# Loading q in rows of eight tokens and sorting it by 0/1 matmuls, in a decayed attention followed by a two-layer network

## The chip, the cores and the metric

The kernel runs on one core of one Trainium2 chip. A core has TensorE (PE, matmuls; its weight loads are listed apart as PEld), VectorE (DVE), ScalarE (ACT), GpSimd (POOL) and SyncE (SP). Each of them takes its own instructions in order; POOL and SP also issue the transfers between the chip's memory and the core's. The metric is the device time of one execution in microseconds (us). Lower is better.

## The reference

```python
# q, k, v: (4, 8, 768, 64) float32: batch, heads, tokens, head size
gamma = 1.0 - 2.0 ** (-5.0 - np.arange(H))
for t in range(S):
    state = gamma[None, :, None, None] * state + np.einsum('bhd,bhe->bhde', k[:, :, t], v[:, :, t])
    y[:, :, t] = scale * np.einsum('bhd,bhde->bhe', q[:, :, t], state)
x = y.transpose(0, 2, 1, 3).reshape(B * S, H * D)      # (3072, 512)
h = x @ w_in                                           # (512, 2048)
s = np.sin(alpha * h)
out = (h + s * s / (alpha + 1e-09)) @ w_out            # (2048, 512)
```

Each head keeps a 64x64 state that fades by its own gamma. Two matrix products with a squared sine between them follow, over all 3,072 tokens.

## The kernel before

**Tiles and groups.** The tokens are cut into 24 tiles of 128, six for each of the four batches. `order` lists them by the order of work: first the first tile of each batch (places 0 to 3, called first to fourth tile here, and e0 to e3 in the code), then the rest. The first four make group 0, then come eight groups of two, and a last one of four. Inside a tile the attention is a masked, decayed product of q and k; between the tiles of a batch it goes through the state. All matmuls read bfloat16.

**One of the first tiles.** Tokens arrive on partitions, as (token, head, 64). `half_T` (line 273) turns q (TH.n.0) and k (TH.n.1) on PE by four 128x128 transposes each, and CH copies the result out of PSUM into `qkT`. `products` (AA, line 299) multiplies k by q in the `pa` banks, `decayed` (E, line 309) multiplies by the table `dec` on DVE, `mixed` (MM, line 339) multiplies by v, and Y copies the result into `xT`, the input of the network. q and k of the very first tile come as float through SP (line 171) and are cast on DVE (cq) and ACT (ck); everything else is cast by POOL's transfers. The fourth tile has the same steps under the names H.0, H.1, A3 and M3.

**One of the fifth to eighth tiles (places 4 to 7).** `stage_T` (T, line 283) turns q and k by 16 transposes on half the columns each, and C copies them out. `burst` (U.n, line 457) is then one block on PE: tile n's part from the state, its own products, the scores of tile n+1 and the sums for the state. What it leaves on DVE is called exit (into `xT`), keep (the state), mask (of the scores); hand is the state's bfloat16 copy on ACT. From the ninth tile (place 8) on, q and k are turned by a DMA transpose that SP issues (X).

**The network.** A slot S.g:m takes a few of the 16 column blocks of w_in: PE multiplies (line 610), ACT takes the sine (line 613), Q squares it (ACT line 618, or DVE line 620), A writes h + s*s/alpha as `gT` on DVE (line 625). S.e:0 to S.e:3 cover the first three tiles in 384 columns, S.e:4 the same four blocks for the fourth tile in 128; the others of group 0 are 512 wide. F.t.f multiplies gT by one block of w_out into the result of tile t (line 635); O copies that out of PSUM and G sends it.

**What sets the order.** The front, up to the end of group 1's first product, is written out by hand: each word of `PLAN` (line 16) issues one step, and each engine gets its instructions in that order. L loads a tile's q, k or v, K a piece of w_in, W a piece of w_out, all from POOL; x and w are matmuls on zeros that fill PE's time; D makes a decay table on POOL out of `qg`, which gr makes on ACT; V scales v. Later groups are issued by loops that the change doesn't touch.

**Banks.** PSUM has four banks in rotation for most uses (`mm`), a pair for products (`pa`) and a pair called `two`, which holds in turn the first mixed results and alpha (`front`), the fourth tile's turned q and k, the results of the first two tiles (until their O), and the bursts.

## Time and profile before

| | |
|---|---|
| median of 3 runs | 209.41 us (208.93 to 209.41) |
| span of the profiled execution, first to last instruction | 206.7 us |
| PE busy | 200.4 us, 97% |
| DVE, ACT, POOL busy | 154.9, 151.6 and 123.6 us |
| PE in 0 to 5, 5 to 10, 10 to 15, 15 to 20 us | 3.81, 4.51, 4.49 and 4.79 us |
| transfers issued by POOL | 80,080 packets, 13.38 MB |

The profiled execution's own time is given as its span; the difference of 2.7 us to the runs' median lies before its first and after its last instruction. PE counts as busy also while it multiplies zeros: in the first 14 us 54 such matmuls take 8.3 us. A line number is one of the kernel before.

### The profile page before, as it was taken

What the parts mean: (1) busy time and instruction counts of PE and PEld (TensorE: products, weight loads), DVE (VectorE), ACT (ScalarE), POOL (GpSimd) and SP (SyncE); (2) the same over time, 40 slices, a digit from 0 to 9 for tenths busy, and PEclk for the clock granted to TensorE, in tenths of its full rate; (3) what the DMA queues carried; (4) which work ended last, traced back from release to release, by engine and by line L of the source; (5) the groups of instructions that cost most, each with busy time, mean ns of one, the idle gap of its engine ahead of it and who ended that gap; (6) DMA issues with size and microseconds to landing.
All of it is one profiled execution on the core that took longest, in us unless ns stands there. A gap on an engine that the chain in (4) does not pass through costs nothing.

```text
span 206.7 us, 5872 instructions
## 1 busy us (share of the span) xinstructions
PE 200.4 (97%) x2399; PEld 126.2 (61%) x2399; DVE 154.9 (75%) x325; ACT 151.6 (73%) x310; POOL 123.6 (60%) x171
## 2 busy tenths in 40 slices
PE   7999999999999999999999999999999999999993
PEld 7545544467776666666666676766766654444463
DVE  5777499878999988878889686976977875656120
ACT  7778788547897787687687788588687679998001
POOL 8998997999979986699485929972310000000000
PEclk9999999999999999999999999999999999999999
DMA  9999999999999999999994998992423101010212
GB/s 135 147 171 192 200 202 173 167 128 134 246 142 146 101 152 190 167 130 138 189 159 67 125 134 108 142 135 53 105 71 35 54 15 38 3 51 0 102 59 96
DMA packets 102907, 24.81 MB, mean 120 GB/s; under 512 B 93360, under 2 KB 99936, under 8 KB 102880
## 3 DMA queue, kind: packets, MB, share of 16 engines
q0 software_dynamic: 80080, 13.38, 90.1%
q1 hardware_dynamic: 22656, 10.99, 25.5%
q8 instruction: 19, 0.31, 0.6%
q10 hardware_dynamic: 144, 0.07, 0.1%
q14 instruction: 8, 0.07, 0.1%
HBM read 27.30 MB, written 6.29 MB: 163 GB/s over the span
## 4 chain that ended last, share of the span: by engine, by line
PE 87%; POOL 6%; DMA 3%; DVE 1%; ACT 0%; issue 0%; POOLq 0%
PE po L635 39%; PE ph L610 38%; DMA w_out<-in_moe_w_out_dram 3%; POOL qkr L125 3%; POOL vr L125 2%; PE poh L662 2%; PE py L372 2%; PE pa L387 1%; PE pt L290 1%; PE py L445 1%; PE py L436 1%; POOL w_in L161 1%; DVE s L620 1%; PE pa L394 1%; PE pa L420 1%; PE y L436 1%
## 5 line engine op out<-in xcount | busy, mean ns | idle before, releaser
L625 DVE SCALAR_TENSOR_TENSOR gT<-s,rec_alpha,ph 128x256 bf16<-128x256 f32 (+3 forms) x164 | 79.7, 522 | 27.2 <-ACT s L618 26.8
L610 PE MATMUL ph<-xT,w_in 128*128 128x256 bf16 (+3 forms) x656 | 98.3, 291 | 0.0
L613 ACT ACTIVATE s<-ph,alpha_sb 128x256 f32<-128x256 f32 (+3 forms) x164 | 76.1, 507 | 27.1 <-PE ph L610 23.7
L635 PE MATMUL po<-w_out,gT 128*128 128x512 bf16 x368 | 94.6, 379 | 0.1
L610 PEld LDWEIGHTS <-w_in 128*128 128x128 bf16 x656 | 63.2, 98 | 32.7 <-DVE s_f L568 0.5
L618 ACT ACTIVATE s<-s 128x512 f32<-128x512 f32 (+1 forms) x93 | 58.3, 627 | 2.9
L635 PEld LDWEIGHTS <-gT 128*128 128x128 bf16 x368 | 34.3, 98 | 30.2 <-DVE gT L625 0.5
L149 POOL DMA_DIRECT2D qk_seq<-in_q_dram x32 | 21.7, 719 | 5.3 <-DMA v_seq<-in_v_dram 3.9
L149 POOL DMA_DIRECT2D qk_seq<-in_k_dram x32 | 21.3, 706 | 4.7 <-DMA qk_seq<-in_q_dram 4.7
L649 DVE COPY o_sb<-po 128x512 f32<-128x512 f32 x20 | 13.8, 689 | 9.2 <-PE po L635 8.8
L149 POOL DMA_DIRECT2D v_seq<-in_v_dram x24 | 16.9, 782 | 0.0
L188 POOL TENSOR_TENSOR v_seq<-v_seq,kgq 128x512 bf16<-128x512 bf16 x9 | 9.3, 1051 | 4.5 <-DMA v_seq<-in_v_dram 4.5
L125 POOL DMA_DIRECT2D vr<-in_v_dram x11 | 10.3, 939 | 0.9 <-DMA w_in<-in_moe_w_in_dram 0.7
L406 DVE TENSOR_TENSOR aTw<-pa,maskq 128x768 bf16<-128x768 f32 x10 | 9.6, 956 | 0.0
L682 PE MATMUL spare<-warm 128*128 128x112 bf16 (+1 forms) x54 | 8.3, 323 | 1.2 <-DVE warm L198 1.2
L494 DVE TENSOR_TENSOR xT<-py,qg 128x512 bf16<-128x512 f32 x13 | 8.9, 684 | 0.5 <-PE py L452 0.5
L666 ACT COPY o_sb<-poh 128x256 f32<-128x256 f32 (+1 forms) x2 | 0.6, 320 | 11.7 <-PE poh L662 11.7
L520 POOL CAST s_q<-s_f 128x256 bf16<-128x256 f32 x1 | 0.4, 398 | 14.2 <-DVE s_f L514 14.2
L390 DVE TENSOR_TENSOR aT<-pa,mask 128x1024 bf16<-128x1024 f32 x7 | 8.5, 1218 | 0.4 <-PE pa L387 0.4
L520 ACT CAST s_q<-s_f 128x256 bf16<-128x256 f32 x12 | 4.8, 396 | 3.4 <-DVE s_f L514 2.7
L125 POOL DMA_DIRECT2D qkr<-in_k_dram x7 | 6.2, 891 | 0.4 <-DMA w_in<-in_moe_w_in_dram 0.4
L125 POOL DMA_DIRECT2D qkr<-in_q_dram x7 | 6.4, 915 | 0.1
(123 smaller groups left out, 178.3 us busy)
## 6 DMA issues: line engine op xcount, KB each, us to landing
out_dram<-o_sb SPq DMA_DIRECT2D x23, 256.0 KB, 3.1
w_in<-in_moe_w_in_dram POOLq DMA_DIRECT2D x8, 256.0 KB, 8.1
w_out<-in_moe_w_out_dram POOLq DMA_DIRECT2D x8, 256.0 KB, 8.0
vr<-in_v_dram POOLq DMA_DIRECT2D x11, 128.0 KB, 6.5
v_seq<-in_v_dram POOLq DMA_DIRECT2D x16, 80.0 KB, 5.0
qkr<-in_q_dram POOLq DMA_DIRECT2D x7, 128.0 KB, 6.2
qkr<-in_k_dram POOLq DMA_DIRECT2D x7, 128.0 KB, 6.1
qk_seq<-in_q_dram POOLq DMA_DIRECT2D x16, 48.0 KB, 4.5
```

The source lines that it names most:

```text
L125: nc.gpsimd.dma_start(out=t, in_=chunk_of(src, j))
L149: nc.gpsimd.dma_start(out=o, in_=src[bt, head(b, m, e), now[0] * C:(now[-1] + 1) * C, :].rearrange("(f i) d -> i f d", i=64))
L188: eng.tensor_mul(t, t, by[:, j % NCH, :, None].to_broadcast([128, H, D]))
L390: return {"mask": lambda: nc.vector.tensor_mul(aT.rearrange("p e n t -> p (e n) t"), pa.rearrange("p e (n t) -> p (e n) t", n=NP), mask_bc)}
L406: return {"mask": lambda: nc.vector.tensor_mul(aT, pa[:, :, 0:384].rearrange("p e (m t) -> p e m t", m=2), maskq[:, None, None, :].to_broa ...
L494: nc.vector.tensor_mul(o, st["pyw", old][:, :, 0:256].rearrange("p b (m t) -> p b m t", m=2), by)
L610: nc.tensor.matmul(self.ph[:, m, :], w_in[:, i, f * 128:(f + 1) * 128], xT[g][:, i, self.lo:self.hi], start=(m == 0 and i == 0), stop=(i = ...
L613: nc.scalar.activation(out=self.s[:, m, :], in_=self.ph[:, m, :], func=ACTF.Sin, scale=alpha_sb[:, f:f + 1])
L618: nc.scalar.activation(out=self.s, in_=self.s, func=ACTF.Square)
L625: nc.vector.scalar_tensor_tensor(gT[self.g][:, f, self.lo:self.hi], self.s[:, m, :], rec_alpha[:, f:f + 1], self.ph[:, m, :], op0=ALU.mult ...
L635: nc.tensor.matmul(po[g, ts], gT[g][:, f, ts * C:(ts + 1) * C], w_out[:, f, :], start=(f == 0), stop=(f == FF - 1))
L649: nc.vector.tensor_copy(o_sb, po[g, ts])
```

## The change

*Loads.* q of the second to eighth tile (`order[1:8]`) is read so that a partition holds eight tokens of one head, one run of 2 KB in memory, where it held one token of eight heads in runs of 256 bytes: 128 runs for a tile instead of 1,024. v of the first tile is read as float by SP behind q and k, and cast on DVE (cv).

*Sorting.* In that layout a transpose alone would leave the tokens out of order. `rows_T` multiplies each of the eight token rows by columns of the identity, once for even and once for odd heads: 16 matmuls of 64 columns, into a whole bank of float. The copy out of PSUM puts the tokens in order. In `stage_T` q and k now have a bank and a copy each.

*Order and engines.* The zeros are 30 and 9 matmuls instead of 41 and 13. The second and third tile's k is copied by ACT, not DVE; the second tile's Y goes from ACT to DVE; `qg` is one product on DVE (ge) and one exponential on ACT; alpha has a bank of its own, and the second tile's products use `two`. Much of PLAN stands in another order.

```diff
+    in_rows = {("q", j) for j in order[1:8]}
...
+    def rows_of(t, j):
+        b, c = divmod(j, NCH)
+        return t[b, :, c * C:(c + 1) * C, :].rearrange("h (i r) d -> h i (r d)", r=H)
...
-            if name != "v" and spread(j):
+            if (name, j) in in_rows:
+                nc.gpsimd.dma_start(out=t.rearrange("p r d -> p (r d)"), in_=rows_of(src, j))
+            elif name != "v" and spread(j):
...
-    for name, src in (("q", q), ("k", k)):
+    for name, src in (("q", q), ("k", k), ("v", v)):
...
+    def rows_T(j, bank=None, apart=False):
+        if bank is None:
+            bank = psum.tile([128, 512], F32, name="pt", tag="mm", bufs=4)
+        pt = bank.rearrange("p (r h i) -> p r h i", r=H, h=NP)
+        for r in range(H):
+            for e in range(2):
+                if apart:
+                    pick = ident.rearrange("p (m e b i) -> p e b m i", m=2, e=2, b=2)[:, e]
+                    o = pt[half(e), r].rearrange("p (b m) i -> p b m i", b=2)
+                else:
+                    pick, o = ident.rearrange("p (h e i) -> p e h i", e=2, i=16)[:, e], pt[half(e), r]
+                nc.tensor.matmul(o, raw["q", j][:, r, :], pick, start=(r == 0), stop=True, skip_group_check=True)
+        o = st["qkT", j][:, :NP, :].rearrange("p h (i r) -> p h i r", r=H)
+        x = pt.rearrange("p r h i -> p h i r")
+        return lambda by: by.copy(o, x) if by is nc.scalar else by.tensor_copy(o, x)
...
     def stage_T(j, tag):
...
-        for i in range(2):
-            for p in range(NP):
-                for e in range(2):
-                    h = 4 * (p % 2) + 2 * e + p // 2
-                    nc.tensor.transpose(pt[half(e), i * NP + p, :], raw["qk"[i], j][:, h, :], ident)
-        return lambda by: by.copy(qkT, pt) if by is nc.scalar else by.tensor_copy(qkT, pt)
+        of_q = rows_T(j, banks[0], apart=True)
+        pt = banks[1].bitcast(BF16)[:, :512].rearrange("p (h t) -> p h t", h=NP)
+        for p in range(NP):
+            for e in range(2):
+                nc.tensor.transpose(pt[half(e), p, :], raw["k", j][:, 4 * (p % 2) + 2 * e + p // 2, :], ident)
+        return of_q, lambda by: by.copy(qkT[:, NP:], pt) if by is nc.scalar else by.tensor_copy(qkT[:, NP:], pt)
...
-    def grow(p):
-        nc.scalar.activation(out=qg[:, 0, p, :], in_=tio, func=ACTF.Exp, scale=lgp[:, p:p + 1], bias=cscale)
+    def grow():
+        nc.scalar.activation(out=qg[:, 0], in_=qg[:, 0], func=ACTF.Exp, bias=cscale)
+    def exponents():
+        nc.vector.tensor_mul(qg[:, 0], tio[:, None, :].to_broadcast([128, NP, C]),
+                             lgp[:, :, None].to_broadcast([128, NP, C]))
...
-L.0.v L.1.q L.1.k L.1.v L.2.q L.2.k L.2.v K.0.0 K.0.1 tk x.41 cq TH.0.0 CH.0.0.D ck w.2 dm TH.0.1 CH.0.1.A kg st
+L.1.q L.1.k L.2.q L.2.k L.1.v L.2.v x.30.112 K.0.0 K.0.1 tk cq.D TH.0.0 ge CH.0.0.D dm.1 w.1 w.3 kg ck.A dm.0
...
```

POOL's first loads, before (a tile's load is 128 partitions of 8 heads of 64; the last number after x is how often the row comes):

```order
L125 DMA vr<-in_v_dram 128x8x64
L125 DMA qkr<-in_q_dram 128x8x64
L125 DMA qkr<-in_k_dram 128x8x64
L125 DMA vr<-in_v_dram 128x8x64
L125 DMA qkr<-in_q_dram 128x8x64
L125 DMA qkr<-in_k_dram 128x8x64
L125 DMA vr<-in_v_dram 128x8x64
L161 DMA w_in<-in_moe_w_in_dram 128x4x256 x2
```

and with the change:

```order
L128 DMA qkr<-in_q_dram 128x1x512
L133 DMA qkr<-in_k_dram 128x8x64
L128 DMA qkr<-in_q_dram 128x1x512
L133 DMA qkr<-in_k_dram 128x8x64
L133 DMA vr<-in_v_dram 128x8x64 x2
L169 DMA w_in<-in_moe_w_in_dram 128x4x256 x2
```

Six loads stand ahead of w_in instead of seven; two of them are q in rows; both v come after both k.

DVE from q of the first tile to the third tile's xT, before (L779 is the cast of q, L281 a copy of turned q or k, L314 and L317 the decay, L352 Y):

```order
L779 CAST qb<-o_sb 128x512
L281 COPY qkT<-pt 128x512
L788 TENSOR_TENSOR dec<-dec,mask_114 128x1024
L314 TENSOR_TENSOR aT<-pa,dec 128x1024
L281 COPY qkT<-pt 128x512
L234 MEMSET lgq 64x1 x8
L235 TENSOR_TENSOR expoq<-tok,lgq 128x48
L314 TENSOR_TENSOR aT<-pa,dec 128x1024
L281 COPY qkT<-pt 128x512
L317 TENSOR_TENSOR aT<-pa,dec 128x2x256 x2
L352 CAST xT<-front 128x2x128
L352 CAST xT<-pyh 128x2x128
```

and with the change, from behind the cast of q (L724 is ge, L785 the cast of v, L314 a copy, L352 and L355 the decay, L390 Y):

```order
L724 TENSOR_TENSOR qg<-tio,lgp 128x512
L314 COPY qkT<-pt 128x512
L833 TENSOR_TENSOR dec<-dec,mask_117 128x512 x2
L785 CAST vr<-o_sb 128x512
L352 TENSOR_TENSOR aT<-pa,dec 128x1024
L246 MEMSET lgq 64x1 x8
L247 TENSOR_TENSOR expoq<-tok,lgq 128x48
L352 TENSOR_TENSOR aT<-pa,dec 128x1024
L355 TENSOR_TENSOR aT<-pa,dec 128x2x256
L390 CAST xT<-pyh 128x4x128
L355 TENSOR_TENSOR aT<-pa,dec 128x2x256
L390 CAST xT<-pyh 128x2x128 x2
```

The two copies of k have left DVE; ge, a cast and the second tile's Y have come to it, the last between the two halves of the third tile's decay.

DVE around the bursts U.4 and U.5, before (L514 is keep, L390 mask, L649 the copy O.1, L497 and L494 exit):

```order
L514 TENSOR_TENSOR s_f<-s_f,py_712 128x128
L514 TENSOR_TENSOR s_f<-s_f,py_713 128x128
L390 TENSOR_TENSOR aT<-pa,mask_114 128x1024
L649 COPY o_sb<-po 128x512
L497 TENSOR_TENSOR xT<-py_712,qg 128x2x128
L497 TENSOR_TENSOR xT<-py_713,qg 128x2x128
L494 TENSOR_TENSOR xT<-py,qg 128x2x2x128
```

and with the change (L535 and L532 are exit, L552 keep, L428 mask, L687 O.1, L328 the copy of the seventh tile's k, C.k6):

```order
L535 TENSOR_TENSOR xT<-py_759,qg 128x2x128
L535 TENSOR_TENSOR xT<-py_760,qg 128x2x128
L552 TENSOR_TENSOR s_f<-s_f,py_759 128x128
L552 TENSOR_TENSOR s_f<-s_f,py_760 128x128
L428 TENSOR_TENSOR aT<-pa,mask_117 128x1024
L687 COPY o_sb<-po 128x512
L328 COPY qkT<-pt 128x512
L532 TENSOR_TENSOR xT<-py,qg 128x2x2x128
```

The exit of U.4 now stands first instead of behind O.1, and the copy of the seventh tile's k is on DVE behind O.1.

98 lines of the change are left out of this document (58 added, 40 removed).

## The prediction

> **What bounds the kernel now.** I read the table of stretches first (time, then busy time of PE, PEld, DVE, ACT and POOL with their instructions, granted clock, DMA share, GB/s), then the chain of waits, then PE and DVE in order of time.
>
> ```profile
> 20.00:25.00 5.00, 4.93 (x35) 2.80 (x36) 2.09 (x7) 3.89 (x10) 4.98 (x7) 1.00 1.36 200
> ...
> 50.00:60.00 10.00, 9.52 (x174) 7.36 (x172) 9.72 (x22) 8.96 (x21) 10.00 (x14) 1.00 1.86 201
> ```
>
> From 20 us on PE is busy all the time, save 0.48 us after 50. The later part gets shorter only if PE has less to do; the part before 20 us, only if that state begins earlier. What begins it, by the chain of waits (start, length, what):
>
> ```profile
> 13.01 7.02 DMA w_out<-in_moe_w_out_dram
> 20.07 0.81 PE po L635 x3
> ...
> 22.42 3.45 PE ph L610 x16
> ```
>
> Read alone this says loads: the second piece of w_out is issued at 13.01 and lands at 20.03. But the chain names only the last of several. DVE and PE in order of time (start, length, line, operation; in brackets the idle time before, and what ended it) show a second chain that ends as late:
>
> ```profile
> 3.97 0.49 DVE L779 CAST qb<-o_sb 128x512 bf16<-128x512 f32 x1 [0.48 <-DMA o_sb<-in_q_dram]
> ...
> 7.63 1.23 DVE L314 TENSOR_TENSOR aT<-pa,dec 128x1024 bf16<-128x1024 f32 x1 [0.41 <-PE pa L305]
> ...
> 9.83 1.22 DVE L314 TENSOR_TENSOR aT<-pa,dec 128x1024 bf16<-128x1024 f32 x1
> ...
> 12.16 1.29 DVE L317 TENSOR_TENSOR aT<-pa,dec 128x512 bf16<-128x512 f32 x2 [0.50 <-PE pa L305]
> ...
> 13.84 0.43 DVE L352 CAST xT<-pyh 128x256 bf16<-128x256 f32 x1
> ...
> 16.28 0.43 DVE L281 COPY qkT<-fourth 128x512 bf16<-128x512 bf16 x1 [1.10 <-PE fourth L279]
> 16.62 0.61 DVE L625 SCALAR_TENSOR_TENSOR gT<-s,rec_alpha,ph 128x384 bf16<-128x384 f32 x1
> 17.18 0.43 DVE L281 COPY qkT<-fourth 128x512 bf16<-128x512 bf16 x1
> 18.16 1.23 DVE L314 TENSOR_TENSOR aT<-pa,dec 128x1024 bf16<-128x1024 f32 x1
> ```
>
> ```profile
> 1.19 3.77 PEld L682 LDWEIGHTS <-warm 128*128 128x128 bf16 x41 [1.19 <-DVE warm L198]
> ...
> 5.42 0.87 PE L682 MATMUL spare<-warm 128*128 128x512 bf16 x2
> 6.12 0.39 PE L279 MATMUL pt<-ident,kb 128*128 128x128 bf16 x4
> 6.35 0.59 PE L682 MATMUL spare<-warm 128*128 128x512 bf16 x2
> ...
> 14.18 1.46 PE L610 MATMUL ph<-xT,w_in 128*128 128x384 bf16 x8
> 15.84 0.40 PE L279 MATMUL fourth<-ident,qkr 128*128 128x128 bf16 x4 [0.20 <-DMA qkr<-in_q_dram]
> 17.72 0.40 PE L305 MATMUL pa<-qkT 64*128 64x128 bf16 x8
> ...
> 20.72 1.05 PE L610 MATMUL ph<-xT,w_in 128*128 128x128 bf16 x16
> ```
>
> Tiles 0, 1, 2 are decayed on DVE at 7.63, 9.83 and 12.16; xT of the third is whole at 13.84 + 0.43 = 14.27. PE's first two 384-wide slots are through at 15.46 (14.18 + 8 x 0.16). Then the fourth tile's q, its copy, a gT step, the copy of k, products at 17.72, decay at 18.16 to 19.39, mix, xT, and the 128-wide slot S.e:4 at 20.72. The next 512-wide slots need that xT, so an earlier w_out alone wins nothing: S.e:4 must come earlier too.
>
> **The change part by part.** *Loads.*
>
> ```profile
> 1.37 1.07 POOL L125 DMA_DIRECT2D vr<-in_v_dram  x1 [0.17 <-issue]
> 2.44 0.89 POOL L125 DMA_DIRECT2D qkr<-in_q_dram  x1
> ...
> 7.65 1.55 POOL L161 DMA_DIRECT2D w_in<-in_moe_w_in_dram  x2
> ...
> 11.42 0.72 POOL L165 DMA_DIRECT2D w_out<-in_moe_w_out_dram  x1
> ```
>
> A load of 1,024 short rows costs POOL 0.89, w_in's 512 rows 0.78 (1.55 / 2), w_out's 256 rows 0.72; on that line 128 rows cost about 0.69 (bounds: 0.5 and 0.89). v of the first tile leaves POOL. POOL then starts w_in at 1.37 + 0.86 + 0.87 + 0.68 + 3 x 0.87 = 6.39 instead of 7.65 (0.86 is 0.69 plus the 0.17 by which the first issue is dearer), and after the fourth tile's q the lead is 1.26 + 0.2 = 1.46: w_out's second piece lands at about 18.6. Bounds of the lead: 0, if the DMA engines set the pace alone, and 1.5. The new wait of POOL is the decay table D.3 behind K.1.0; it needs qg from ACT (about 12.7 by the chain below; one exponential 512 wide in place of four) when POOL is there (13.0), and behind it stand pieces needed after 20 us. v as float is a third transfer on SP; its cast costs DVE 0.49 as q's does and is read at about 11 us, so even 3 us of delay is covered.
>
> *Sorting.*
>
> ```profile
> L324 PE MATMUL ps<-vr,kb 128*64 128x64 bf16 x8 | 0.3, 195 | 0.0
> L290 PE MATMUL pt<-ident,qkr 128*64 128x128 bf16 x64 | 2.5, 222 | 0.0
> 37.03 0.64 PE L290 MATMUL pt<-ident,qkr 128*64 128x128 bf16 x16
> L281 DVE COPY qkT<-pt 128x512 bf16<-128x512 bf16 x3 | 1.3, 422 | 1.4 <-PE pt L279 1.4
> L649 DVE COPY o_sb<-po 128x512 f32<-128x512 f32 x20 | 13.8, 689 | 9.2 <-PE po L635 8.8 <-ACT o_sb L647 0.4
> L352 ACT CAST xT<-front 128x512 bf16<-128x512 f32 x2 | 1.2, 584 | 0.4 <-PE front L348 0.4
> ```
>
> Per tile q takes 16 matmuls of 64 columns on 128x64 weights instead of 4 (first tiles) or 8 (later) transposes. The nearest row is L324, same weights and columns: 8 in 0.29 of which one takes 0.195, so (0.29 - 0.195) / 7 = 0.0136 each, 0.22 for 16. The eight transposes it replaces in a later tile: L290 ran 16 in 0.64 (one of them 0.222), (0.64 - 0.222) / 15 = 0.028 each, 0.22 for 8. So the later four tiles cost nothing more; the upper bound, 16 at L290's 0.028, is 0.22 a tile, 0.9 in all. I take 0, since L324 has the very shape.
>
> [...]
>
> The copy reads float PSUM across 256-byte steps: on ACT the nearest float row is 0.58, as for bf16; on DVE 0.69 against 0.42. I take these; twice them is the upper bound.
>
> *The chain to the third tile's xT.* Line by line from the new order, with these prices and 0.04 from one engine to the next. q's cast ends at 4.46, and its transposes no longer wait for 41 fillers (until 4.96): they start at 4.50. Four 512-wide fillers instead of two then stand ahead of k's transposes. The filler rows give 0.43 each at 5.42 and about half at 6.35, so PE's pace doubles near 6.0; k's transposes start at 6.35 instead of 6.12. DVE has meanwhile the exponents (0.69), q's copy, the mask of dec in two halves and v's cast (0.49), done by 7.4; they hide in the idle time before its first decay, and lengthen it by what they pass 7.8. Copy on ACT 6.78-7.37, products, first decay **7.85** (before 7.63). q of the second tile: sorted 7.75-8.15, ACT 8.19-8.78, k's copy to 9.26, products from 9.30, second decay **9.74** (9.83). Third tile: q's copy 9.26-9.85, alpha, k's copy 10.08-10.67, products, first half of the decay at **11.15** (12.16): its products no longer wait for a bank, and DVE has given both k copies to ACT. Then Y.1 11.79-12.48, second half 12.38-13.06, Y.2.1 13.44-**13.87** (14.27). PE runs half of S.e:1 early and is through with both slots at **14.87** (15.46).
>
> *The fourth tile.* Its q lands at 15.84 - 1.26 = 14.6, so it no longer waits (15.84: 0.20 for the load). But what comes behind it is late next:
>
> ```profile
> 15.09 0.58 ACT L613 ACTIVATE s<-ph,alpha_sb 128x384 f32<-128x384 f32 x1 [1.32 <-PE ph L610]
> 15.71 0.52 ACT L618 ACTIVATE s<-s 128x384 f32<-128x384 f32 x1
> ```
>
> ACT's order is now sine, sine, square, square: sines at 14.43 and 15.07, squares at 15.69 and 16.20. DVE's H.0 copy 15.31-16.0; gT waits for the square, 16.25; H.1's copy stands behind it in the queue, 16.78-17.21; products 17.25, decay **17.69** (18.16), mix 18.97, xT 20.0, S.e:4 at **20.04** (20.72). Of the 0.68, one F matmul of 0.215 has moved behind S.e:4: gain 0.46. With fillers that cost nothing it would be 0.7; without the lead of the loads, 0.
>
> *From 37 us.* From T.4 to U.5 PE has the same work in both orders: 22 F matmuls, three tiles' transposes, Z's scores, U.4.
>
> ```profile
> 42.27 0.49 DVE L514 TENSOR_TENSOR s_f<-s_f,py 128x128 f32<-128x128 f32 x2 [0.61 <-PE py L452]
> 42.68 1.22 DVE L390 TENSOR_TENSOR aT<-pa,mask 128x1024 bf16<-128x1024 f32 x1
> 44.29 0.69 DVE L649 COPY o_sb<-po 128x512 f32<-128x512 f32 x1 [0.40 <-ACT o_sb L647]
> 44.90 0.75 DVE L497 TENSOR_TENSOR xT<-py,qg 128x256 bf16<-128x256 f32 x2
> ...
> 45.11 0.31 PE L372 MATMUL py<-qkT,s_q 64*64 64x128 bf16 x8
> ...
> 50.83 0.31 PE L372 MATMUL py<-qkT,s_q 64*64 64x128 bf16 x8 [0.48 <-DVE qkT L291]
> ```
>
> Before, U.5 started when O.1's copy had freed its bank (44.29 + 0.69), and the exit of U.4 came after. Now exit (0.75), keep (0.49) and the mask (1.22) stand ahead of O.1's copy, and C.k6's copy behind it: with U.4 4.4 after T.4, O.1's copy ends 8.26 after T.4, C.k6's 8.60; U.5 goes from 8.07 (45.11 less 37.03) to 8.35, and its scores wait 0.1 more. In return T.7 now stands ahead of S.1:1 and S.1:2, and its k copy is half as long: U.6 comes at 13.92 instead of 13.80. So the stall of 0.48 at 50.83 is not gained but moved to U.5: 0.1 lost. If DVE is ahead there by 0.4, it is 0.4 gained. SP's first transpose, X.8, now follows one output instead of standing ahead of three; in the rows above no engine waits for SP, so I cost it at nothing.
>
> **Sum:** -0.46 + 0.1 + 0 (sorting) = -0.36: span 206.7 to 206.35. The median of the runs, 209.41, is 2.7 above the profiled span; I keep that: **209.0**. A change within 0.3% (0.63 us) can't be told from none.
>
> **Rivals.** *The loads decide alone*: S.e:4 follows w_out, and 1.25 to 1.46 of lead arrive. For it: POOL's row of issues without a pause. Against: the chain through DVE has 0.68 less, not 1.4. It decides if ACT's squares and DVE's copies come early. Less 1.3 and 0.1 back: 208.2.
>
> *PE's pace doubles later* (the slower side). PE now rests from 4.0 to 4.5, and this falls into the time in which it was busy without a break before its pace doubled near 6.0. If the doubling comes a like time later, about 9.4: fillers +0.38, k's transposes +0.24, products and the next tile's 16 matmuls +0.2 each, so the second decay comes 1.0 late, and S.e:4 at about 21.1, 0.4 (plus the moved F, 0.2) later than before: 209.4 + 0.6 + 0.1 = 210.1. It decides from the moment the fillers behind q still take 0.43 at 6.1.
>
> [...] The granted clock in the stretches reads 1.00 from the start, so only the spacing shows it here.
>
> *The sorting costs PE what L290's row costs*: 0.9 in the part that PE bounds, after the gain in front: 209.41 - 0.36 + 0.9 = 209.9, no change to tell. For it: weights are loaded 16 times where they were loaded 8 times. Against: L324. [...]
>
> **How the numbers follow.** Forecast as summed 0.45 (own range 208.6 to 209.5, a third of it below 208.78); loads alone 0.22; late doubling 0.18; dear sorting 0.15. Faster: 0.15 + 0.2 + 0.02 = 0.37. Slower: half of the late doubling, and 0.08 from dear sorting with a lost gain: 0.17. The rest 0.46. The range, from the loads' case with 0.4 won at U.5 to the late doubling: 207.8 to 210.2.
>
> **What would show it.** Right: a second decay near 9.7 and a third near 11.2; the fourth tile's q copied before 16.0 with gT behind it near 16.25; S.e:4 near 20.0; w_out's second piece landed near 18.6; U.5 waiting for the copy of O.1 or of C.k6; 24 sorted and transposed instructions in 0.6 us. Wrong: S.e:4 before 19.6 (the loads decide); first decay after 8.3 (the doubling); PE idle time at T.4 and T.5, or more than 0.8 us for their 24 instructions.

## The result

The changed kernel takes 211.87 us (median of four executions, 210.58 to 212.08), the kernel before 209.41 us (208.93 to 209.60) on the same chip. The ratio is 1.012, its interval 1.008 to 1.016: slower, by 2.5 us, where no change was forecast as likeliest. The profiled execution took 211.73 us, with a span of 209.6 us where the kernel before has 206.7. A profile is of one execution, and executions of one kernel here differ by 1 to 2% (25 of the kernel before on one chip 207.69 to 210.22, ten of the version with 41 fillers 209.23 to 213.26), so below the medians say what a kernel takes, and a trace says where.

The same views as before, of the changed kernel. DVE in order of time (start, length, line, operation, then the idle time before and what ended it), up to the fourth tile's decay:

```profile
4.09 0.81 DVE L785 CAST qb<-o_sb 128x512 bf16<-128x512 f32 x1 [0.80 <-DMA o_sb<-in_q_dram]
...
8.93 0.43 DVE L785 CAST vr<-o_sb 128x512 bf16<-128x512 f32 x1 [1.70 <-DMA o_sb<-in_v_dram]
9.28 1.22 DVE L352 TENSOR_TENSOR aT<-pa,dec 128x1024 bf16<-128x1024 f32 x1
...
11.96 1.22 DVE L352 TENSOR_TENSOR aT<-pa,dec 128x1024 bf16<-128x1024 f32 x1 [0.99 <-PE pa L343]
...
13.88 0.69 DVE L355 TENSOR_TENSOR aT<-pa,dec 128x512 bf16<-128x512 f32 x1 [0.70 <-PE pa L343]
...
20.43 1.23 DVE L352 TENSOR_TENSOR aT<-pa,dec 128x1024 bf16<-128x1024 f32 x1
```

PE in order of time:

```profile
1.19 2.98 PE L718 MATMUL spare<-warm 128*128 128x112 bf16 x30 [1.19 <-DVE warm L209]
4.96 0.61 PE L312 MATMUL pt<-ident,qb 128*128 128x128 bf16 x4 [0.79 <-DVE qb L785]
5.36 1.91 PE L718 MATMUL spare<-warm 128*128 128x512 bf16 x4
7.07 0.63 PE L312 MATMUL pt<-ident,kb 128*128 128x128 bf16 x4
8.38 0.61 PE L343 MATMUL pa<-qkT 64*128 64x128 bf16 x8 [0.68 <-ACT qkT L314]
...
13.25 0.59 PE L343 MATMUL pa<-qkT 64*128 64x128 bf16 x8
...
22.82 1.05 PE L648 MATMUL ph<-xT,w_in 128*128 128x128 bf16 x16
```

ACT's cast of k; and on POOL the issue that runs while q is cast, the first piece of w_in, and the load that waits behind it:

```profile
5.95 0.62 ACT L785 CAST kb<-o_sb 128x512 bf16<-128x512 f32 x1 [1.11 <-DMA o_sb<-in_k_dram]
```

```profile
3.72 0.93 POOL L133 DMA_DIRECT2D qkr<-in_k_dram  x1
...
6.34 1.55 POOL L169 DMA_DIRECT2D w_in<-in_moe_w_in_dram  x2
...
9.64 0.91 POOL L133 DMA_DIRECT2D qkr<-in_k_dram  x1 [0.65 <-DMA qkr<-in_k_dram]
```

And the loads of the first 20 us by destination (number, size, median us from issue to landing), before and with the change:

```profile
qkr<-in_q_dram POOLq DMA_DIRECT2D x3, 128.0 KB, 4.8
o_sb<-in_k_dram SPq DMA_DIRECT2D x1, 256.0 KB, 3.9
```

```profile
qkr<-in_q_dram POOLq DMA_DIRECT2D x3, 128.0 KB, 6.8
o_sb<-in_k_dram SPq DMA_DIRECT2D x1, 256.0 KB, 4.7
```

The front lost its time before 17 us. POOL reached w_in at 6.34, as forecast (6.39), but the tiles' q that it loads land 2.0 us later after their issue than before (6.8 for 4.8), k and v 2.4 and 2.1 us. The cast of v waited for its load until 8.93, and the first decay stands right behind it in DVE's queue. In this execution the cast held the decay by little: the products end at 8.99 (8.38 + 0.61), so the decay could have begun near 9.03 at the earliest. PE's fillers still take 0.43 each (1.91 for four) after 5.36, and eight products still take 0.59 at 13.25: PE's pace doubled only behind that.

| start of (us) | before | forecast | with the change | late against before |
|---|---|---|---|---|
| first decay | 7.63 | 7.85 | 9.28 | 1.65 |
| second decay | 9.83 | 9.74 | 11.96 | 2.13 |
| third decay | 12.16 | 11.15 | 13.88 | 1.72 |
| fourth decay | 18.16 | 17.69 | 20.43 | 2.27 |
| S.e:4 | 20.72 | 20.04 | 22.82 | 2.10 |
| T.4 | 37.03 | | 39.34 | 2.31 |
| U.5 | 45.11 | | 48.18 | 3.07 |
| U.7 | 55.26 | | 58.38 | 3.12 |
| last tile's first output product | 199.61 | | 202.99 | 3.38 |

The two stretches that were shown of before (time, busy time of PE, PEld, DVE, ACT and POOL, granted clock, share of the transfers' engines, GB/s):

```profile
20.00:25.00 5.00, 4.95 (x53) 2.84 (x55) 3.13 (x5) 3.34 (x9) 5.00 (x7) 1.00 1.37 199
...
50.00:60.00 10.00, 9.38 (x193) 7.49 (x194) 8.53 (x18) 8.52 (x20) 9.91 (x14) 1.00 1.80 153
```

PE is as full from 20 us on as before (4.95 for 4.93), and has lost 0.14 more in 50 to 60. So 2.1 us of the loss are there at S.e:4, another 0.8 comes between T.4 and U.7. From the last row to the end it takes 0.45 less than before, so the span grows by 2.9. The middle, by engine (PE, then DVE, then POOL in order of time):

```profile
39.34 0.44 PE L297 MATMUL pt<-ident,qkr 128*64 128x64 bf16 x16
39.62 0.39 PE L327 MATMUL pt<-ident,qkr 128*64 128x128 bf16 x8
...
48.18 0.31 PE L410 MATMUL py<-qkT,s_q 64*64 64x128 bf16 x8 [0.60 <-DVE o_sb L687]
```

```profile
43.55 1.78 DVE L199 TENSOR_TENSOR vr<-vr,kg 128x512 bf16<-128x512 bf16 x1
...
47.45 0.67 DVE L687 COPY o_sb<-po 128x512 f32<-128x512 f32 x1
```

```profile
43.67 1.10 POOL L199 TENSOR_TENSOR vr<-vr,kg 128x512 bf16<-128x512 bf16 x1
```

The sorted q and the transposed k of a tile take 0.67 (39.34 to 40.01) for 24 instructions; the 16 transposes before took 0.64. U.5 waits 0.60 for O.1's copy, the wait that the prediction named. The scaling of v at 43.55 is new: it takes 1.78 where 0.69 stood before.

### The profile page after: what moved, and what is told of

It reads as the page before. It is cut to its first block, busy times and chain, and to the rows that moved or that the text cites. A ratio compares the mean times of both kernels' runs of the same rounds, so it can differ in the third digit from the quotient of the medians.

```text
span 209.6 us, 5947 instructions
## 1 busy us (share of the span) xinstructions
PE 198.5 (95%) x2422; PEld 126.6 (60%) x2452; DVE 156.3 (75%) x329; ACT 151.3 (72%) x310; POOL 120.5 (57%) x170
## 3 DMA queue, kind: packets, MB, share of 16 engines
q0 software_dynamic: 73664, 13.25, 82.4%
## 4 chain that ended last, share of the span: by engine, by line
PE 88%; DVE 5%; issue 3%; DMA 2%; ACT 1%
PE ph L648 39%; PE po L673 35%; PE poh L700 2%; DMA o_sb<-in_q_dram 2%; PE py L410 1%; PE spare L718 1%; DVE aT L428 1%; PE pt L297 1%; PE pt L312 1%; PE pa L343 1%; DVE o_sb L687 1%; PE py L474 1%; PE py L483 1%; DVE aT L355 1%; PE pa L425 1%
## 5 line engine op out<-in xcount | busy, mean ns | idle before, releaser
L673 PE MATMUL po<-w_out,gT 128*128 128x512 bf16 x344 | 90.3, 379 | 2.6 <-issue 2.1
L687 DVE COPY o_sb<-po 128x512 f32<-128x512 f32 x20 | 13.7, 687 | 8.8 <-PE po L673 8.8
L133 POOL DMA_DIRECT2D vr<-in_v_dram x10 | 9.1, 912 | 1.0 <-DMA w_in<-in_moe_w_in_dram 1.0
L532 DVE TENSOR_TENSOR xT<-py,qg 128x512 bf16<-128x512 f32 x13 | 8.9, 683 | 0.8 <-PE py L490 0.8
L428 DVE TENSOR_TENSOR aT<-pa,mask 128x1024 bf16<-128x1024 f32 x7 | 8.5, 1216 | 0.0
L718 PE MATMUL spare<-warm 128*128 128x112 bf16 (+1 forms) x37 | 6.3, 357 | 1.2 <-DVE warm L209 1.2
L615 POOL CAST s_q<-s_f 128x512 bf16<-128x512 f32 x2 | 1.4, 702 | 9.6 <-DVE s_f L610 9.6
```

What stands on the lines that cost most here:

```text
L133: nc.gpsimd.dma_start(out=t, in_=chunk_of(src, j))
L428: return {"mask": lambda: nc.vector.tensor_mul(aT.rearrange("p e n t -> p (e n) t"), pa.rearrange("p e (n t) -> p (e n) t", n=NP), mask_bc)}
L532: nc.vector.tensor_mul(o, st["pyw", old][:, :, 0:256].rearrange("p b (m t) -> p b m t", m=2), by)
L673: nc.tensor.matmul(po[g, ts], gT[g][:, f, ts * C:(ts + 1) * C], w_out[:, f, :], start=(f == 0), stop=(f == FF - 1))
L687: nc.vector.tensor_copy(o_sb, po[g, ts])
```

## The experiments

The kernel before has medians of 207.66 to 209.41 in the sets of runs here, which are of several chips, so each kernel is compared with the kernel before on its own chip; the ratio is theirs, with its 95% interval. "S.e:4" and landing times are from the profiled execution of each.

### Fillers and the load of v

From these views I held the pace of PE and the load of v on SP for the causes. Three edits of the changed kernel, alone and together, and one of the kernel before:

```diff
-... L.2.v x.30.112 K.0.0 ...
+... L.2.v x.41.112 K.0.0 ...                     (41 fillers)
-L.1.q L.1.k L.2.q L.2.k L.1.v ...  CH.0.1.A cv.D AA.0.pa
+L.1.q L.1.k L.2.q L.2.k L.0.v L.1.v ...  CH.0.1.A AA.0.pa   (first v by POOL, none on SP)
```

> The changed kernel with 41 narrow fillers again instead of 30, nothing else. Two causes are on the table for the 2.1 us by which S.e:4 came later: PE's pace doubles only near 13 us (the fillers behind q still take 0.43 each, and PE rested from 4.2 to 5.0), and the third float load on SP, which brings k of the first tile 0.8 late and holds DVE's queue until v lands at 8.9. Pace theory: doubling before 8 us, first decay still near 9.3 because DVE waits for v, second near 10.9 instead of 11.96, S.e:4 near 21; median 210.0 to 210.6. SP theory: nothing moves, 211.5 to 212.

> The changed kernel with v of the first tile loaded by POOL as bfloat16 again (behind the second q and k), without SP's float load and DVE's cast; 30 fillers stay. SP theory: k of the first tile is cast at 5.2 instead of 5.95, the first decay comes at 8.0 instead of 9.28 and all behind it 1.2 earlier: 210.3 to 210.8. Pace theory: the cold fillers keep k's transposes at 7.07, the first decay gains only the 0.25 it stood behind v's cast, 211.3 to 211.8.

> Both edits: 41 fillers, and v of the first tile by POOL. If each of the two holds the first decay at about the same time, only both together free it. Both theories: first decay near 7.8, second near 9.8, S.e:4 near 20.2, as the prediction had it; 209.2 to 209.9, with what is lost at U.4 to U.6 (0.8 in the trace). If a third cause is in front, S.e:4 stays after 21 and the time above 210.3.

> The kernel before with 30 narrow fillers instead of 41, nothing else. Pace theory: PE rests before q's transposes, the pace doubles one or two steps later, the second decay moves from 9.83 to past 10.5; 210.2 to 211.5, and runs that differ among themselves by up to 2 us. SP theory: 41 fillers only delayed q's transposes, so no change: 209.2 to 209.6.

Measured: 41 fillers 210.03 us, ratio 1.006 (1.0015 to 1.0105); v by POOL 211.59, 1.013 (1.009 to 1.017); both 209.66, 1.004 (1.001 to 1.007); the kernel before with 30 fillers 209.11, 1.000 (0.997 to 1.004). Neither edit alone mends the change (41 fillers take back about half of the loss), and fewer fillers alone don't harm the kernel before by more than 0.4%. The trace with 41 fillers is of an execution of 212.63, one of the longest of ten; it shows that more fillers don't secure the pace: PE had doubled its pace by 5.4, then rested and lost it again.

```profile
5.39 1.03 PE L718 MATMUL spare<-warm 128*128 128x512 bf16 x4
8.23 0.40 PE L312 MATMUL pt<-ident,kb 128*128 128x128 bf16 x4 [1.81 <-ACT kb L785]
9.31 0.61 PE L343 MATMUL pa<-qkT 64*128 64x128 bf16 x8 [0.68 <-ACT qkT L314]
```

k of the first tile had landed 6.3 us after its issue, PE rested 1.81 us, and from 9.31 on eight products take 0.61.

### Rows of eight tokens in front

A third suspect: the 2-KB rows of q first in POOL's queue hold back SP's 256-byte runs of k. Edits of the version with 41 fillers and v by POOL, the third moving only two scalings of v late in POOL's queue:

```diff
-    in_rows = {("q", j) for j in order[1:8]}
+    in_rows = {("q", j) for j in order[4:8]}       (rows47)
-L.1.q L.1.k L.2.q L.2.k L.0.v L.1.v
+L.0.v L.1.q L.1.k L.2.q L.2.k L.1.v                (vfirst)
-V.6.P L.7.v ...  V.7.P L.10.q L.10.k
+L.7.v V.6.P ...  L.10.q V.7.P L.10.k               (vmoved)
```

> The third version (41 fillers, first v by POOL) with q of the second to fourth tile again in rows of one token; only the fifth to eighth tile are sorted. Theory (2-KB rows ahead in POOL's queue hold back the 256-byte runs of SP's loads): the float k of the first tile lands 3.9 us after its issue, as in the kernel before (4.6 with the rows), its cast starts by 5.3, the first decay by 7.7 (8.05), the third tile's by 11.2 (11.45), the fourth tile's q no longer lands 6.5 us after its issue but near 5, and S.e:4 starts near 20.1; time about 0.4 below the third version. Rival one (it is POOL's order, q and k of two tiles ahead of v, whatever their rows): k lands at 4.6 again, S.e:4 near 20.6, time as the third version's. Rival two (chance from run to run): landing anywhere between 4 and 6.

> The third version (41 fillers, first v by POOL, q of seven tiles in rows of eight tokens) with v of the first tile first in POOL's queue again, as in the kernel before. Theory (2-KB rows hold back the 256-byte runs): part of it stays, since the first rows now start 1.07 later: k lands 4.0 to 4.4 us after its issue (4.6), cast at 5.3 to 5.7. Rival one (POOL's order alone): 3.9, cast at 5.2, first decay by 7.7, the same as before. Rival two (chance): between 4 and 6. Time within 0.4 of the third version's in all cases.

> The third version (41 fillers, first v by POOL, all seven tiles in rows) with POOL's scaling of v of the seventh and eighth tile one load later in POOL's queue each. Theory (a DVE operation with both inputs in SBUF stands still while POOL runs its own TENSOR_TENSOR): in the third version the square on DVE at 49.35 took 1.62 instead of 0.69 beside POOL's scaling at 49.31 to 50.41; moved, the square takes 0.69, the stall of 0.47 ahead of U.6 is gone, U.4 to U.7 takes 13.7 (14.15), and the time is 0.4 below the third version's. Rival (DVE is late there by its own list): the square takes 0.69, yet U.6 waits as long and U.4 to U.7 stays above 14.0.

Measured: without the rows 208.83, 1.0005 (0.997 to 1.004), S.e:4 at 20.36, k landing in 4.2; v first 209.12, 1.003 (1.000 to 1.007), 20.77, k in 4.3; scalings moved 209.40, 1.002 (0.999 to 1.006), 20.59, k in 3.9. The last one has the very front of the version it was made from, where k took 4.6, so k's landing moves from execution to execution, and a difference of 0.7 between two traces proves nothing. Over all traces k takes 3.9, 3.9, 4.2, 4.4 and 3.9 without rows in front and without v on SP, and 4.6, 3.9, 4.3, 5.9, 4.9 and 4.2 with rows: a tendency, not shown.

The moved scalings did what was expected of them. DVE and POOL of the version with 41 fillers and v by POOL, and then DVE with the scalings moved:

```profile
49.35 1.62 DVE L658 TENSOR_TENSOR s<-s 128x512 f32<-128x512 f32 x1 [0.53 <-ACT s L651]
```

```profile
49.31 1.10 POOL L199 TENSOR_TENSOR vr<-vr,kg 128x512 bf16<-128x512 bf16 x1
```

```profile
49.37 0.69 DVE L658 TENSOR_TENSOR s<-s 128x512 f32<-128x512 f32 x1 [0.53 <-ACT s L651]
```

The square takes 0.69 again, no stall is left ahead of U.6 (0.47 before the edit), and from U.4 to U.7 it takes 13.61 us instead of 14.15. The theory is that DVE, with both inputs in SBUF, stands still while POOL runs its own product: in the changed kernel V.5's 1.78 is 0.68 and the whole 1.10 of POOL's. An operation with an input from PSUM kept its length beside POOL's product: the mask at 43.75 took 1.22 in the version with 41 fillers and v by POOL, beside POOL's of 1.04 at 43.54, and 1.22 at 47.60 with none beside it.

### The sorting alone, and the scalings set apart

```diff
 the changed kernel's code and loads of q, with the kernel before's PLAN: 41 fillers,
 L.0.v first, gr as ge on DVE and one exponential; C.4.D becomes C.k4.D C.q4.A, and so on   (order)
-V.6.P L.7.v ...  V.7.P L.10.q ...  (14, (4, 6))
+L.7.v V.6.P ...  L.10.q V.7.P ...  (14, (4, 5))      (apart: in order, and in the kernel before)
```

> The sorting alone: q of the second to eighth tile in rows of eight tokens and its 0/1 matmuls, but the order of the kernel before everywhere: 41 fillers, v of the first tile by POOL and first in its queue, the later tiles' steps where they stood. Theory (sorting is free on PE, and the reordered front with 30 fillers made the loss): first decay at 7.6 to 7.9, S.e:4 at 20.3 to 20.8, from T.4 to U.7 18.0 to 18.3 (before 18.23), time 207.9 to 208.5 where the kernel before has 208.2, ratio 0.998 to 1.002. Rival (rows of eight tokens hold back the other loads, or the sorted copies come late): first decay after 8.0 or S.e:4 after 21.0, ratio 1.003 and more.

> The sorting alone in the old order, and three scalings of v set apart: POOL's of the seventh and eighth tile one load later each, DVE's of the fifteenth tile one step earlier. Theory (a DVE operation on SBUF alone stands still while POOL runs TENSOR_TENSOR): no DVE operation on SBUF alone takes over 0.9 anywhere after 37 us, no stall ahead of U.6, U.4 to U.7 13.3 to 13.5 (before 13.95), time 0.3 to 0.6 below the sorting alone, about 207.7, ratio 0.996 to 0.999. Rival (the coincidences only move): one such operation over 1.2 stays, and the time is within 0.2 of the sorting alone.

> The kernel before with the same three scalings of v set apart and nothing else. Theory: the square on DVE near 48.8 takes 0.69 instead of 1.33, the stall of 0.48 ahead of U.6 is gone, time 0.3 to 0.5 lower, ratio 0.9975 to 0.9985. Rival: U.6 waits as before, ratio within 0.999 to 1.001.

> The changed kernel itself once more, beside the others on this chip and in many executions. Theory (its 30 fillers and the float load of v on SP make the front late in every execution): no time below 210, ratio 1.010 to 1.020, first decay after 9.0, at or behind the cast of v. Rival (chance: k's landing and the doubling of PE's pace fall differently from execution to execution): a third or more of the times below 209.8, ratio below 1.008, or a profile with the first decay before 8.5.

Measured: sorting in the old order 210.94, 1.010 (1.006 to 1.014), far from what I expected; with the scalings apart 210.35, 1.008 (1.005 to 1.011), where I expected 0.996 to 0.999 and no long operation of DVE, yet its square at 50.47 still took 1.48 beside POOL's product at 50.28; the kernel before with them apart 208.24 against 208.44, 0.998 (0.995 to 1.001), not to be told from no change, though its trace has lost the stall of 0.48 ahead of U.6; the change again 211.41, 1.010 (1.005 to 1.016), with one of six executions at 209.70 where I expected none below 210.

The old order doesn't suit the sorting, for a reason that the prediction didn't have. PE in the version "order", at the seventh tile:

```profile
44.48 0.44 PE L297 MATMUL pt<-ident,qkr 128*64 128x64 bf16 x16
45.72 0.41 PE L327 MATMUL pt<-ident,qkr 128*64 128x128 bf16 x8 [0.79 <-ACT qkT L300]
```

A sorted q fills a bank of float by itself, so a tile takes two of the four banks in rotation where both halves shared one. Two of them hold U.4's results until exit.4, which in the old order stands behind O.1; so T.6's k has no bank until ACT has copied T.6's own q, and from U.4 to U.5 it takes 5.0 us, not 3.8. That the bank is what k lacks is read from the kernel's text; the trace shows the wait of 0.79 for ACT's copy. The changed order, with exit.4 first, makes this room, at the price of the wait on O.1: there the 24 instructions of T.6 run without a break. The rest of that version's loss is 0.65 at S.e:4 (k landed in 4.9) and 0.7 at 104 us, where DVE scales v beside POOL; with the scalings apart that last part is gone.

The change once more, in another execution, with k early (5.03) and the pace doubled before 5 us: the first decay waits for v all the same, then PE for the second tile's k and for alpha, and the pace falls back.

```profile
8.56 0.43 DVE L785 CAST vr<-o_sb 128x512 bf16<-128x512 f32 x1 [1.55 <-DMA o_sb<-in_v_dram]
8.90 1.22 DVE L352 TENSOR_TENSOR aT<-pa,dec 128x1024 bf16<-128x1024 f32 x1
```

```profile
9.13 0.40 PE L312 MATMUL pt<-ident,qkr 128*128 128x128 bf16 x4 [1.27 <-DMA qkr<-in_k_dram]
10.71 0.20 PE L854 MATMUL pal<-ident_f,alpha_row 16*128 16x16 f32 x1 [1.18 <-DMA alpha_row<-in_moe_alpha_dram]
10.84 0.64 PE L297 MATMUL pt<-ident,qkr 128*64 128x64 bf16 x16
```

### One part at a time

Landing times told the kernels apart: with v on SP, the q, k and v that POOL loads in front take 6.3 to 7.4 us (medians of each trace), in all others 4.7 to 6.0. Four runs were to show what v on SP, the rows and the fillers do alone:

```diff
 the kernel before:  -for name, src in (("q", q), ("k", k)):   -L.0.v L.1.q     -w.2 AA.0
                     +for ... ("k", k), ("v", v)):             +L.1.q           +w.2 cv AA.0    (v on SP)
 the changed kernel: in_rows of order[4:8]                                      (after_rows47)
 v by POOL, no rows in front, x.30.112                                          (rows47_x30)
 the changed kernel: in_rows of order[4:8], x.41.112                            (rows47_x41)
```

> The kernel before with one edit: v of the first tile leaves POOL and is read as float by SP, third in its queue, and cast by DVE ahead of the first products; 41 fillers, all of q in rows of one token, nothing sorted. Theory (the third float load on SP's queue holds up all loads of the front, as in the three traces that have it: 6.6 to 7.4 us from issue to landing against 4.8 to 6.0 in the others): alpha lands 5.5 to 7 us after its issue (3.8), the second tile's loads 6.5 to 7.3 (4.8 to 5.1), v is cast at 8.2 to 9.0, the first decay starts at 8.6 to 9.4 (7.63), S.e:4 at 21.8 or later (20.72), ratio 1.006 to 1.015. Rival (it is the rows of eight tokens, or the order): landings near 5, v cast by 7.5, first decay by 8.1, S.e:4 by 21.1, ratio below 1.003.

> The changed kernel with q of the second to fourth tile again in rows of one token; float v on SP, 30 fillers and the new order stay. Theory (v on SP): landings of the front stay at 6.5 to 7.4 us, v is cast at 8.2 to 9.0, first decay at 8.6 to 9.6, S.e:4 after 22.0, ratio 1.009 to 1.016 like the change. Rival (the rows of eight tokens in front): k lands in 3.9 to 4.4, the other loads in about 5, first decay by 8.2, ratio below 1.006.

> The version with the first v by POOL and sorting in the fifth to eighth tile alone, with 30 fillers instead of 41. Theory (30 fillers cost something only where loads of the front are late, since PE's rest then grows): k lands by 4.4, first decay by 8.2, S.e:4 by 20.6, time as with 41 fillers (ratio 0.999 to 1.003). Rival (30 fillers alone delay the doubling of PE's pace): fillers still at 0.43 after 6.5, first decay after 8.6, ratio 1.006 and more.

> The changed kernel with q of the second to fourth tile in rows of one token and 41 narrow fillers; float v on SP and the new order stay. It is the last of the eight combinations of fillers (30, 41), v (SP, POOL) and rows in front (yes, no). Theory (30 fillers turn any lateness of the loads into a rest of PE, 41 cover it): the front's loads land 6.3 to 7.3 us after their issue as in every trace with v on SP, yet PE rests less than 1 us between the narrow fillers and k's transposes, first decay 8.2 to 9.2, ratio 1.002 to 1.007, between 1.0155 (30 fillers) and 1.0005 (v by POOL). Rival (v on SP is dear in the new order whatever the fillers): ratio 1.010 and more, S.e:4 after 22.0.

They took 208.78, 211.29, 208.69 and 211.03 us. Loads in the kernel before with v on SP, grouped as above:

```profile
qkr<-in_q_dram POOLq DMA_DIRECT2D x3, 128.0 KB, 6.3
alpha_row<-in_moe_alpha_dram SPq DMA_DIRECT2D x1, 8.0 KB, 5.5
```

The one edit makes the other loads of the front later: q of the next tiles 6.3 us from issue to landing where it was 4.8, alpha 5.5 for 3.8. That half of the theory held. How the loads of the two queues share the transfers' engines was not shown. But the time doesn't follow: ratio 1.001 (0.998 to 1.004). The first decay is 0.40 late (8.03), the second 0.88, S.e:4 only 0.25 (20.97): in the old order most of it is made up.

The three others complete a table of the new order (ratios, with S.e:4 of the trace):

| first v | rows in front | 30 fillers | 41 fillers |
|---|---|---|---|
| SP | yes | 1.012 and 1.010; 22.82 and 23.07 | 1.006; 24.09 (execution of 212.63) |
| SP | no | 1.0155 (1.0095 to 1.022); 23.24 | 1.016 (1.008 to 1.024); 21.34 (and 23.08 with the edit of the last experiment) |
| POOL | yes | 1.013; 21.65 | 1.004; 20.57 |
| POOL | no | 1.0015 (0.998 to 1.005); 21.43 (execution of 209.94) | 1.0005; 20.36 |

Each place is the trace of one execution, and k's landing is in it: 5.9 and 3.9 with v by POOL and 30 fillers, 6.3 in the 24.09. S.e:4 is later with v on SP in all four pairs, by 1.0 to 3.5. Without rows, v on SP is dear with either number of fillers, so my condition (41 cover it) fell, though the last experiment takes 1.0% of the 1.016 away. With v by POOL, no rows and 30 fillers I expected S.e:4 by 20.6; PE was at full pace from 7.81 on there, and waited 1.11 us for a tile's v and 0.75 for the fourth tile's q. What v on SP does where PE's pace is full throughout, with 41 fillers and no rows (DVE, then PE, in order of time):

```profile
8.00 0.59 DVE L785 CAST vr<-o_sb 128x512 bf16<-128x512 f32 x1 [0.95 <-DMA o_sb<-in_v_dram]
8.52 1.20 DVE L352 TENSOR_TENSOR aT<-pa,dec 128x1024 bf16<-128x1024 f32 x1
```

```profile
8.92 0.40 PE L312 MATMUL pt<-ident,qkr 128*128 128x128 bf16 x4 [0.96 <-DMA qkr<-in_k_dram]
...
9.90 0.40 PE L312 MATMUL pt<-ident,qkr 128*128 128x128 bf16 x4 [0.43 <-DMA qkr<-in_q_dram]
...
10.90 0.40 PE L312 MATMUL pt<-ident,qkr 128*128 128x128 bf16 x4 [0.26 <-DMA qkr<-in_k_dram]
...
21.34 1.05 PE L648 MATMUL ph<-xT,w_in 128*128 128x128 bf16 x16 [0.19 <-ACT xT L390]
```

v is cast at 8.00 and the decay stands behind it; then PE waits three times for loads, and S.e:4 is 0.98 later than with v by POOL (20.36). That is the loads' part in this trace.

With 30 fillers and the same loads S.e:4 is at 23.24, and there PE's pace has fallen. Stretches of that trace (time, busy time of PE, PEld, DVE, ACT and POOL, granted clock, share of the transfers' engines, GB/s):

```profile
4.00:7.00 3.00, 1.40 (x10) 0.53 (x8) 2.59 (x5) 1.57 (x6) 3.00 (x5) 1.00 1.70 173
7.00:15.00 8.00, 6.37 (x64) 3.78 (x65) 3.89 (x14) 3.98 (x13) 6.57 (x10) 0.57 2.08 171
15.00:20.00 5.00, 4.35 (x34) 2.39 (x33) 3.84 (x10) 4.78 (x10) 3.98 (x6) 1.00 1.57 192
```

PE had been at full pace at 4.5, rested 1.42 us for k, and had a granted clock of 0.57 over the 8 us from 7 on; if it stood at half in the fall and at 1.00 otherwise, that is an estimated 6.9 us at half (8 x 0.43 / 0.5). S.e:4 is 1.9 us later than in the trace before. The lost pace is the likely reason for most of it; k landed 1.4 us later too (5.3 for 3.9), and no run sets the two apart.

### Keeping PE busy, and the cast later

```diff
 the changed kernel: -dm.1 w.1 w.3 kg   -TH.1.0 w.1 CH.1.0.A TH.1.1 CH.1.1.A
                     +dm.1 w.1 w.7 kg   +TH.1.0 w.5 CH.1.0.A TH.1.1 w.4 CH.1.1.A    (filled)
 and besides         -CH.0.1.A cv.D AA.0.pa   -E.1.- CH.2.1.A
                     +CH.0.1.A AA.0.pa        +E.1.- cv.D CH.2.1.A                  (cast later)
```

> The changed kernel with twelve more 512-wide fillers where PE rested: four ahead of k's transposes, eight around the second tile's; v on SP, 30 narrow fillers, rows and order stay, so the loads are as late as before. Theory (late loads let PE rest for over a microsecond, and then its pace falls back to half): pace stays full from 7 us on (16 sorted matmuls in 0.44, products in 0.40), first decay still at 8.9 to 9.4 behind v's cast, the second at 10.8 to 11.3 (11.96 to 12.37), S.e:4 at 21.3 to 21.9 (22.82 to 23.07), ratio 1.005 to 1.010. Rival (the loads alone set the front): pace full, yet second decay at 11.8 or later and S.e:4 after 22.4, ratio 1.010 and more.

> The same twelve fillers, and v's cast on DVE behind the second decay instead of ahead of the first. Theory (DVE's queue stands behind v's cast): first decay at 8.0 to 8.8, as soon as its products are there, second at 10.0 to 10.8, v's cast by 12.0, S.e:4 0.3 to 0.8 earlier than with the fillers alone, near 21.0, ratio 1.003 to 1.008. Rival (the products are as late as v): first decay within 0.2 of the run with the fillers alone, S.e:4 too.

Measured: 212.59, ratio 1.020 (1.012 to 1.028), and 213.50, 1.024 (1.019 to 1.030). Both missed. The pace was full from 4.4 in the first, but k took 6.2, and eight fillers, 2.1 us, stood ahead of matmuls that could have gone: the second decay came at 13.15. In the second PE had no rest at all between 4.96 and 9.4, and its pace stayed half:

```profile
4.96 0.61 PE L312 MATMUL pt<-ident,qb 128*128 128x128 bf16 x4 [0.80 <-DVE qb L785]
5.37 3.62 PE L718 MATMUL spare<-warm 128*128 128x512 bf16 x8
```

So fillers are no cure: those behind a wait cost what they take, and 4.4 us of work without a break didn't double the pace at once. Whether the later cast helps can't be read from it, since k's transposes, at 8.78, came at the time of v's landing.

### The coincidence at 104 us

The version with v on SP, 41 fillers and no rows had a ratio of 1.016 with only 1.0 us lost at S.e:4. Its trace lost 1.5 us more at one place. DVE and POOL there, and DVE with one scaling moved:

```diff
-    for i, spot in (..., (14, (4, 6))):
+    for i, spot in (..., (14, (4, 5))):
```

> The version before this one (v on SP, 41 fillers, no rows of eight in front) with one edit far from the front: DVE's scaling of the fifteenth tile's v one step earlier. In that version's trace it took 2.78 us at 105.29 instead of 0.68, beside POOL's three scalings from 105.41 on, and the lag against the other traces grew by 1.5 us there. Theory (DVE on SBUF alone stands still beside POOL's TENSOR_TENSOR, and this coincidence is 1.5 of the 2.4 us): the scaling takes 0.7 to 0.9, no lag is added between 95 and 115 us, span about 207.3, ratio 1.005 to 1.011 instead of 1.0161. Rival (the loads in front make all of it, and the coincidence is covered by other work): ratio 1.014 or more.

```profile
105.29 2.78 DVE L199 TENSOR_TENSOR v_seq<-v_seq,kgq 128x512 bf16<-128x512 bf16 x1
```

```profile
105.41 3.56 POOL L199 TENSOR_TENSOR v_seq<-v_seq,kgq 128x512 bf16<-128x512 bf16 x3
```

```profile
104.11 0.91 DVE L199 TENSOR_TENSOR v_seq<-v_seq,kgq 128x512 bf16<-128x512 bf16 x1
```

Measured: 209.50, ratio 1.006 (1.003 to 1.008), from 1.016 (1.008 to 1.024, four executions). The trace is of an execution of 211.26, in which the pace fell back at 11 us, so its span says little; but the scaling takes 0.91, and its steps are as late at 120 us as at 95. The 1.5 us of the one trace are 0.7%, so the fall of 1.0% holds some chance too. What stays, 0.6%, is about the 1.0 us that the front lost in the trace at full pace; in this one S.e:4 came at 23.08.

## Why the prediction was wrong

**The step that failed** is the front's term of the sum, -0.46 with S.e:4 at 20.04. It came at 22.82, 2.10 later than before. Three statements under that term were wrong.

*"read at about 11 us, so even 3 us of delay is covered"*: this counted v's own landing against the first matmul that reads it. It left out two things. The transfer is not alone: as SP's third load it makes the other loads of the front late, 6.3 for 4.8 us in the single edit. And the cast stands on DVE ahead of the first decay. How much that second part costs differs: the first decay began 1.4 us after its products ended in the repeat of the change, 1.0 after with 41 fillers and no rows, 0.3 after in the first trace, and 0.04 after, so not held at all, in three others.

*"PE's pace doubles near 6.0"*: in the first trace of the change it doubled behind 13.25, and there PE made most of the delay: k's transposes began at 7.07 (forecast 6.35) without a rest ahead of them, and the products and all steps up to the third tile's products ran at half pace.

*"q's cast ends at 4.46"*: it took 0.81 instead of 0.49 and ended at 4.90, beside an issue of POOL that lasts to 4.6 in the new order, where one ended at 4.2 before, so the transposes that fewer fillers were to free began at 4.96 and not at 4.50.

**k's landing** was taken as 5.18 without a word. It lands between 3.7 and 6.3 us after its issue in these traces. In the change's first trace its 0.8 of delay cost nothing by itself, since the fillers at half pace lasted longer. In others this and the late loads let PE rest, and in four traces the pace fell behind such rests.

**The late doubling** was a rival with the right side and the right place, at 0.18 and 210.1. Its condition ("the fillers behind q still take 0.43 at 6.1") came true, and pace doubled behind 13.3 rather than at 9.4. It was priced as a delay of the first doubling alone; that a pace once doubled falls back, as in the trace at 10.84, was not in it. Between the run at full pace (S.e:4 at 21.34) and the others with v on SP (22.82, 23.07, and 23.24 without rows) lie 1.5 to 1.9 us, most of them likely pace; the loads make 1.0 in the run at full pace.

**The lead of the loads** was right at the issue (6.34 for 6.39) and didn't arrive. In the change the fourth tile's q leaves POOL at 8.33, 1.3 early, but the loads of its kind take 6.8 us instead of 4.8. With v by POOL it left at 9.21 and PE waited for it to 15.55, where 14.6 was forecast and 15.84 stood before:

```profile
15.55 0.44 PE L297 MATMUL fourth<-ident,qkr 128*64 128x64 bf16 x16 [0.20 <-DMA qkr<-in_q_dram]
```

So the gain of 0.46 at S.e:4 came to 0.15 there (20.57 for 20.72) and to 0.36 at best. The lower bound in the prediction, no lead because the transfers set the pace, was the right end.

**The sorting** was right as a price on PE: 0.67 for both kinds where 0.64 stood, against the upper bound of 0.22 more a tile. The 16 sorted matmuls of the fourth tile take 0.44 in the change's trace, of which one takes 0.199, so 0.016 each. What it didn't price is the second bank.

**The term from 37 us, +0.1,** was right in the usual case, though not in the change's first trace. U.5 waits for O.1's copy, as forecast. The prediction put U.5 0.28 later, and the wait is 0.28 to 0.29 in the traces of the new order where V.5 has its usual length. From T.4 to U.7 seven of these take 18.17 or 18.18 us, where the kernel before takes 18.23. The change's first trace takes 19.04. Two things that the prediction didn't have make most of these 0.8: V.5 takes 1.8 beside POOL's product, and the wait is 0.60 (0.61 in the one other trace with that meeting); and PE loses about 0.56 within U.6, up to 54.50, as it loses 0.5 in two other traces, which I can't explain. The stall of 0.48 at U.6 was not moved by the order: it stays (0.47 and 0.46) in two traces of the new order in which DVE's square there takes 1.6 beside POOL's product, and is gone where the square is short.

**What stays open:** how much the rows in front cost by themselves (1.004 against 1.0005 with 41 fillers, 1.013 against 1.0015 with 30, the 1.013 with a coincidence of 1.1 us in its trace); what decides when PE's pace doubles; how the 2.1 us at S.e:4 divide between loads and pace; the 0.56 within U.6. No version here beats both kernels beyond doubt: the kernel before with its scalings set apart has 0.998, with 1 inside its interval.

## What to carry to other kernels

A load that is said to be covered has to be followed twice: to whatever stands behind its consumer in that engine's queue (here the first decay, held by up to 1.4 us), and to the other loads that share the transfers with it (here 6.3 us from issue to landing for 4.8). In a stretch where the loads end last, look at landing times from issue, not only at when the issue comes. And when a change shifts everything by a microsecond, look for operations of DVE that now fall beside one of POOL: one such meeting made 1.5 us in a trace, and moving it took that version from 1.016 to 1.006.
